# A bias that VectorE works out in one operation where ScalarE took two, and five changed slots, in a top-k attention and two mixture layers

## The chip, the cores and the metric

The kernel runs on one core of a Trainium2 chip. The metric is the device time of one execution in microseconds, as the median of several runs. Engines are named as in the profile: PE is TensorE, DVE is VectorE, ACT is ScalarE, POOL is GpSimd, SP issues most DMAs.

## The reference, cut to what matters

```python
# q, k, v: (2, 8, 576, 64); top_k 32
scores = scale * np.matmul(q, k.transpose(0, 1, 3, 2))
kth = np.partition(scores, -top_k, axis=-1)[..., -top_k:-top_k + 1]
mask = scores >= kth
scores = np.where(mask, scores, -1000000000.0)
scores = scores - np.max(scores, axis=-1, keepdims=True)
attn = np.exp(scores)
attn = attn / (np.sum(attn, axis=-1, keepdims=True) + 1e-09)
x = np.matmul(attn, v)                      # then to 1152 tokens x 512
...
for e in range(4):                          # first layer, gates p
    out += p[:, e:e + 1] * (np.maximum(x @ w1[e], 0.0) @ w2[e])
...
h = np.maximum(np.maximum(x @ m1, x @ m2), x @ m3)   # second layer
return h @ mo
```

## The kernel before, in words

**Work.** The 1152 tokens are nine tiles of 128 rows. For each tile and each of four pairs of heads there is one "pair" of attention work, 36 in all, numbered n from 0 (tiles 0 to 3 in order, then tiles 4 and 5 mixed, then 6 to 8). A pair has two heads, j = 0 and j = 1. The result of a pair is a slice `xl`, `xh` (a value in two parts) of a tile's `x`, written at lines L630 and L631. Expert work (the first layer, lines L776 to L778, three matmuls for one product) needs whole tiles: stage c of it, for c from 1 to 6, multiplies tiles c-1 and c with half of the first layer's weights, and needs the four slices of tile c.

**One head of one pair.** PE makes the scores (L477 to L489), ACT copies them to `s` (L501). DVE then finds the 32 largest of 576 scores by seven operations, i = 0 to 6: MAX8 (eight largest, L519) for even i, MATCH_REPLACE8 (with a MATCH_VALUE_LOAD, L521) for odd i. `m[:, 0]` is the largest value, `m[:, 31]` the 32nd, which is known after i = 6. The masked exponential is made on ACT for the heads in `ON_ACT`, which are j = 0 of pairs 2 to 35 and j = 1 of pairs 2, 5, 6, 8, 9, 10, 12, 13 and 14: `negate` (L526) puts -scale times the largest into `nb`; `mask` runs a Prelu (L540) that multiplies what lies under the 32nd value's side by a huge or tiny factor, an Identity (L541) that makes the bias `nb` = scale * kth + nb, and the Exp with that bias and a running sum (L542). For the other heads ACT makes the Exp (L533) and DVE or POOL multiplies by the mask (L547). PE transposes the result (`psp`, L565, L570), ACT copies it (`pt`, L568, L573), PE multiplies with v (`psv`, L607, L610). The sums go through `guard` (ACT, L578), `recip` (DVE, L584), `spread` (ACT, L588), a transpose (`psr`, PE, L593) and a copy `r` (ACT, L595). `norm` (DVE, L617) makes `xt`, ACT `xh` (L630), POOL `xl` (L631).

**Order.** The engines run their instructions in program order. The order is written in slots: pair n begins at slot 8n, and a table of options says at which slot after that each step is issued. `stag` is the delay of j = 1 against j = 0, `at` the slots of the two transposes, `lag` the slots between a PE step and the ACT copy of its result, `rec` that of `recip`, `guard` by default one before, `pv` that of the product with v, `turn` that of `trans_r`. BOTH holds for pairs 8, 9, 10, 12, 13 and 14, SECOND for pair 7, THIRD for pair 11, LOOSE for pairs 15 to 35. Top-k operations of a slot are put ahead of the rest of it. Slots are taken as their steps come up, so a slot lasts about two top-k operations on DVE.

**Filling.** Between two slots the program issues expert work for PE up to a planned time: `clock["goal"]` rises by what `dve(n)` adds for each DVE operation (0.07 us and n/960 us). A stage of expert work is not issued before the slot in which its newest tile's last slice is. When no expert work can be issued, the slot passes without any.

Other names that come up: L269 and L275 split weights in two parts (ACT, then POOL or DVE), L921 and L923 do the same for hidden values, L393 and L394 for k.

Of the kernel before, what the change touches and what calls it, by code (L numbers as in the profile page):

```python
# [10 lines left out]
F32 = mybir.dt.float32  # L11
# [3 lines left out]
AF = mybir.ActivationFunctionType  # L15
ALU = mybir.AluOpType
PSUM = bass.MemoryType.PSUM

TOPK = 32
# [19 lines left out]
FIRST = dict(stag=2, new=1, scores=-12, trans=11, pv=17, rec=16, lag=2, sum=4, late=1)  # L39
MIDDLE = dict(stag=2, new=1, scores=-12, at=(11, 12), pv=14, rec=12, lag=1, sum=0, late=1)  # L40
TIGHT = dict(stag=3, new=1, scores=-7, at=(10, 11), guard=11, rec=11, spread=12, pv=12, turn=12, norm=13, split=13, last=14, lag=0, lag_s=1, sum=0, late=1)
SECOND = dict(TIGHT, rec=12, norm=14, split=14, last=15)
THIRD = dict(stag=4, new=1, scores=-4, at=(11, 12), guard=12, rec=13, spread=13, pv=14, turn=14, norm=15, split=15, last=16, lag=0, lag_s=2, sum=0)
BOTH = dict(stag=4, new=1, scores=-4, at=(14, 14), pv=17, rec=15, lag=2, lag_t=1, sum=0, late=1)
LOOSE = dict(stag=4, new=1, scores=-4, at=(14, 14), pv=17, rec=15, split=22, last=24, lag=2, sum=0)

EARLY = 7
SOONER = 3
# [13 lines left out]
def kernel(  # L62
# [14 lines left out]
    nc = tc.nc  # L77
    B, HP, D, _, S = k.shape
    NT, DM = out.shape
    E = gates.shape[2]  # L80
    P = 128
# [6 lines left out]
    SCALE = 1.0 / float(D) ** 0.5  # L88
# [24 lines left out]
    at = ctx.enter_context(tc.tile_pool(name="at", bufs=2))  # L113
# [17 lines left out]
    def dve(n):  # L131
        clock["dve"] += 0.07 + n / 960.0
# [318 lines left out]
    class Pair:  # L451
# [55 lines left out]
        def topk(self, j, i):  # L507
            if i == 0:
                if self.n or j:
                    self.m[j] = at.tile([P, TOPK], F32, tag="m%d" % j, name="m8")  # L510
                self.w[j] = at.tile([P, 2, SH], F32, tag="w%d" % j, bufs=1, name="work")
            assert ("s", j) in self.did
            dve(S)
            if self.n == j == i == 0:
                return
            m, r = self.m[j], i // 2
            src = self.s[j] if i <= 1 else self.w[j]
            if i % 2 == 0:
                nc.vector.max(m[:, 8 * r:8 * r + 8], src)  # L519
            else:  # L520
                nc.vector.match_replace(out=self.w[j], in_to_replace=m[:, 8 * r:8 * r + 8], in_values=src, imm_value=NEG)  # L521

        def negate(self, j):
            m = self.m[j]
            self.nb[j] = at.tile([P, 1], F32, tag="nb%d" % j, name="nb")
            nc.scalar.activation(out=self.nb[j], in_=m[:, 0:1], func=AF.Copy, scale=-SCALE)  # L526

# [7 lines left out]
        def mask(self, j):  # L535
            p = self.p[:, j].rearrange("p (a n) -> p a n", a=2)
            s, kth, total = self.s[j], self.m[j][:, TOPK - 1:TOPK], self.rs[:, j:j + 1]
            if self.on_act[j]:
                eb = self.nb[j]
                nc.scalar.activation(out=s, in_=s, func=AF.Prelu, scale=-1.0, bias=kth, alpha=1.0 / STEEP)  # L540
                nc.scalar.activation(out=eb, in_=kth, func=AF.Identity, scale=SCALE, bias=self.nb[j])  # L541
                nc.scalar.activation(out=p, in_=s, func=AF.Exp, scale=-SCALE * STEEP, bias=eb, accum_out=total)  # L542
                self.did.update([("p", j), ("sum", j)])
                return lambda: None
            if not self.on_pool[j]:
                dve(S)
                nc.vector.scalar_tensor_tensor(out=p, in0=s, scalar=kth, in1=p, op0=ALU.is_ge, op1=ALU.mult, accum_out=total)  # L547
                self.did.update([("p", j), ("sum", j)])
                return lambda: None
            nc.gpsimd.tensor_scalar(out=s, in0=s, scalar1=kth, scalar2=None, op0=ALU.is_ge)  # L550
            nc.gpsimd.tensor_tensor(out=p, in0=p, in1=s, op=ALU.mult)
            self.did.add(("p", j))

            def add():
                nc.scalar.activation(out=s, in_=p, func=AF.Copy, accum_out=total)
                self.did.add(("sum", j))
            return add
# [75 lines left out]
    def attention():  # L633
# [5 lines left out]
        def options(n):  # L639
            return TIGHT if n == HP - 1 else SECOND if n == 2 * HP - 1 else MIDDLE if n in (HP - 2, 2 * HP - 3, 2 * HP - 2) else FIRST if n < 2 * HP else THIRD if n == 3 * HP - 1 else BOTH if n in ON_ACT[1] else LOOSE  # L640

        def at_slot(s, f, *a):
            later.setdefault(s, []).append((f, a))
# [3 lines left out]
        for n, (c, hp, t) in enumerate(pairs):  # L647
# [8 lines left out]
            elif n and t < FULL:  # L656
                o = options(max(0, n - 2))
                at_slot(max(8 * n + options(n)["scores"] - LOAD_FULL, 8 * (n - 2) + o["scores"] + o["stag"] + 1), load_full, n)
        free = {"k": -99, "q": -99}
        for key, n in first_use.items():  # L660
# [3 lines left out]
            load, split = (load_k, split_k) if key[0] == "k" else (load_q, split_q)  # L664
            at = max(s0 + options(n)["scores"] - (SPLIT_K if key[0] == "k" else SPLIT_Q), free[key[0]] + 2)
            if key[0] == "k" and key[1] and key[2]:

                at = max(at, 8 * pairs.index((MIXED, key[2] - 1, MIXED)) + options(n)["scores"] + options(n)["stag"] + (1 if key[2] == HP - 1 else 4))
# [3 lines left out]
        for n, (c, hp, t) in enumerate(pairs):  # L672
            s0 = 8 * n
            prs[n] = Pair(n)
            pr = prs[n]
            o = options(n)
            if n == 2 * HP - 2:
                o = dict(o, guard=11, rec=13, spread=13, turn=14)

            def two(s, f, *a, lag=o["lag"]):  # L680
                if f == pr.scores and n > 2 * HP:
                    at_slot(s, lambda: later.setdefault(s + lag, []).insert(0, (f(*a), ())))
                    return
                at_slot(s, lambda: at_slot(s + lag, f(*a)))
            for j in range(2):
                b0 = s0 + o["stag"] * j
                two(b0 + o["scores"] - SOONER * ((t, hp) in later_scores) - (n == HP - 1 and not j), pr.scores, j, lag=o.get("lag_s", o["lag"]))
                for i in range(7):
                    if o["new"]:
                        later.setdefault(b0 + i, []).insert(0, (pr.topk, (j, i)))  # L690
                    else:
                        at_slot(b0 + i, pr.topk, j, i)
                at_slot(b0 + 2, pr.negate, j)
                at_slot(b0 + 5, pr.exp, j)
                late = o.get("late", MASK_LATE) * pr.on_act[j] + (n == 3 * HP and not j)
                two(b0 + 7 + late, pr.mask, j, lag=o["sum"] if n < EARLY else 3)
                two(s0 + o["at"][j] if "at" in o else b0 + o["trans"] + late + (late > 0), pr.trans_p, j, lag=o.get("lag_t", o["lag"]))
            two(s0 + o["at"][1] if "at" in o else s0 + o["stag"] + o["trans"], pr.trans_p, 2, lag=o.get("lag_t", o["lag"]))
            at_slot(s0 + o.get("guard", o["rec"] - 1), pr.guard)
            at_slot(s0 + o["rec"], pr.recip)  # L700
            if o is LOOSE:
                at_slot(s0 + o["rec"], at_slot, s0 + o["rec"] + 1, pr.spread)
            else:
                at_slot(s0 + o.get("spread", o["rec"] + 1), pr.spread)
            at_slot(s0 + o["pv"], pr.pv)
            two(s0 + o.get("turn", o["rec"] + 2), pr.trans_r)
            end = max(o["pv"], o["rec"] + 2) + o["lag"]
            if n == 1:
                at_slot(s0, nc.sync.dma_start, gate, gates)
            if n == HP - 1:  # L710
                between.setdefault(s0 + o["norm"], []).append((norm_gates, ()))
            if "norm" in o:
                between.setdefault(s0 + o["norm"], []).append((pr.norm, ()))
            else:
                at_slot(s0 + end + 1, pr.norm)
            two(s0 + o.get("split", end + 2), pr.split_x)
# [6 lines left out]
        last = {}  # L723
        for n, p in enumerate(pairs):
            o = options(n)
            last[p[0:2]] = 8 * n + o.get("last", max(o["pv"], o["rec"] + 2) + 2 * o["lag"] + 2)
        for n in range(len(alone)):
            at_slot(ALONE_FROM + ALONE_STEP * n, load_alone, n + 1)
        end = max(last.values()) + 1
        s = min(later)  # L730
        while s <= end:
            todo = later.pop(s, [])
            i = 0
            while i < len(todo):
                f, a = todo[i]
# [15 lines left out]
    lag = []  # L751
# [438 lines left out]
```

## Time and profile before

| | |
|---|---|
| median of the runs | 738.36 us |
| runs | 732.49, 738.36, 738.43 us |
| time of the profiled execution | 732.22 us |
| span of the profiled execution, first to last instruction | 730.4 us |
| granted TensorE clock over the span | 1.000 |
| PE busy (matmul) | 714.1 us, 98% |
| DVE busy | 578.5 us, 79% |
| ACT busy | 504.5 us, 69% |
| POOL busy | 477.7 us, 65% |

The profiled execution took 1.8 us more than its span, and 6.1 us less than the median. Busy shares are averages over the whole span: attention fills DVE until about 430 us, expert work fills PE until the end. Matmuls are pipelined and their ends are modelled, so the waits of an engine say more than its busy share.

### The profile page before, as it was taken

What the parts mean: (1) busy time and instruction counts of PE and PEld (TensorE: products, weight loads), DVE (VectorE), ACT (ScalarE), POOL (GpSimd) and SP (SyncE); (2) the same over time, 40 slices, a digit from 0 to 9 for tenths busy, and PEclk for the clock granted to TensorE, in tenths of its full rate; (3) what the DMA queues carried; (4) which work ended last, traced back from release to release, by engine and by line L of the source; (5) the groups of instructions that cost most, each with busy time, mean ns of one, the idle gap of its engine ahead of it and who ended that gap; (6) DMA issues with size and microseconds to landing.
All of it is one profiled execution on the core that took longest, in us unless ns stands there. A gap on an engine that the chain in (4) does not pass through costs nothing. (4 is left out here: it accounts for less than half of the span.)

```text
span 730.4 us, 13791 instructions
## 1 busy us (share of the span) xinstructions
PE 714.1 (98%) x4758; PEld 637.5 (87%) x4758; DVE 578.5 (79%) x1174; ACT 504.5 (69%) x1127; POOL 477.7 (65%) x416
## 2 busy tenths in 40 slices
PE   6999999999999999999999999999999999999997
PEld 3677688889999998899889998999898998998996
DVE  6999989989999999999999964776879873323441
ACT  4868989899987887788788876566556753442531
POOL 2514878678989976788879777866736763542520
PEclk9999999999999999999999999999999999999999
DMA  8995465545756553555455446886889856543501
GB/s 240 310 273 205 136 207 160 163 123 155 212 151 191 157 170 125 172 165 188 133 154 170 144 122 208 298 285 215 278 256 329 256 182 223 179 125 115 188 1 43
DMA packets 57813, 135.26 MB, mean 185 GB/s; under 512 B 9936, under 2 KB 23120, under 8 KB 57744
## 3 DMA queue, kind: packets, MB, share of 16 engines
q1 hardware_dynamic: 49248, 125.74, 54.7%
q10 hardware_dynamic: 8496, 8.65, 3.4%
q8 instruction: 37, 0.61, 0.3%
q14 instruction: 32, 0.26, 0.1%
HBM read 123.36 MB, written 11.01 MB: 184 GB/s over the span
## 5 line engine op out<-in xcount | busy, mean ns | idle before, releaser
L275 POOL TENSOR_TENSOR wlo<-raw,whi 128x512 fp32r<-128x512 f32 x252 | 332.4, 1348 | 137.5 <-ACT whi L269 120.2
L269 ACT ACTIVATE whi<-raw 128x1024 fp32r<-128x1024 f32 x164 | 169.6, 1057 | 18.3 <-PE ps L778 9.8
L776 PE MATMUL ps<-xl,whi 128*128 128x256 f32 (+1 forms) x584 | 173.7, 297 | 0.5 <-POOL xl L631 0.5
L778 PE MATMUL ps<-xh,wlo 128*128 128x256 f32 (+1 forms) x584 | 170.6, 292 | 0.0
L777 PE MATMUL ps<-xh,whi 128*128 128x256 f32 (+1 forms) x584 | 170.5, 292 | 0.0
L519 DVE MAX8 m<-work 128x8 f32<-128x576 f32 x216 | 154.9, 743 | 0.1
L776 PEld LDWEIGHTS ps<-xl,whi 128*128 128x128 f32 x584 | 110.7, 189 | 1.8 <-POOL xl L631 0.7
L777 PEld LDWEIGHTS ps<-xh,whi 128*128 128x128 f32 x584 | 109.7, 188 | 0.9 <-issue 0.2
L778 PEld LDWEIGHTS ps<-xh,wlo 128*128 128x128 f32 x584 | 109.6, 188 | 0.0
L521 DVE MATCH_REPLACE8 work<-m,work 128x576 f32<-128x576 f32 x144 | 106.5, 740 | 0.0
L275 DVE TENSOR_TENSOR wlo<-raw,whi 128x1024 fp32r<-128x1024 f32 x38 | 54.3, 1436 | 50.1 <-ACT whi L269 37.7
L776 PE MATMUL ps<-wlo,h 128*128 128x512 f32 x224 | 90.3, 403 | 0.0
L778 PE MATMUL ps<-whi,h 128*128 128x512 f32 x224 | 87.7, 392 | 0.0
L777 PE MATMUL ps<-whi,h 128*128 128x512 f32 x224 | 87.7, 391 | 0.0
L245 POOL TENSOR_TENSOR narrow<-narrow,raw 128x256 int32<-128x256 int32 x48 | 46.7, 979 | 21.3 <-DMA narrow<-narrow 5.5
L501 ACT ACTIVATE s<-pss 128x288 f32<-128x288 f32 x128 | 45.8, 405 | 14.2 <-PE pss L481 6.9
L519 DVE MAX8 m<-s 128x8 f32<-128x576 f32 x71 | 53.0, 746 | 1.9 <-ACT s L501 1.9
L521 DVE MATCH_REPLACE8 work<-m,s 128x576 f32<-128x576 f32 x72 | 53.3, 740 | 0.0
L568 ACT ACTIVATE pt<-psp 128x512 f32<-128x512 f32 x72 | 40.0, 599 | 16.6 <-PE psp L565 16.6
L1057 DVE TENSOR_TENSOR tm<-ps,tm 128x384 f32<-128x384 f32 x36 | 19.8, 556 | 39.0 <-PE ps L778 39.0
L778 PEld LDWEIGHTS ps<-whi,h 128*128 128x128 f32 x224 | 42.1, 188 | 9.8 <-POOL h L916 0.3
L776 PEld LDWEIGHTS ps<-wlo,h 128*128 128x128 f32 x224 | 42.7, 191 | 6.6
(118 smaller groups left out, 1493.0 us busy)
## 6 DMA issues: line engine op xcount, KB each, us to landing
raw<-in_w_dram SPq DMA_DIRECT2D x128, 512.0 KB, 4.2
raw<-narrow SPq DMA_DIRECT2D x36, 512.0 KB, 4.3
raw<-in_m_dram SPq DMA_DIRECT2D x36, 256.0 KB, 5.1
whole<-in_w_dram SPq DMA_DIRECT2D x14, 512.0 KB, 5.9
narrow<-narrow ACTq DMA_DIRECT2D x48, 128.0 KB, 5.2
kraw<-in_k_dram SPq DMA_DIRECT2D x16, 288.0 KB, 4.4
raw<-in_mo_dram SPq DMA_DIRECT2D x12, 256.0 KB, 5.6
kfull<-in_k_dram SPq DMA_DIRECT2D x9, 288.0 KB, 5.3
```

The source lines that it names most:

```text
L245: nc.gpsimd.tensor_tensor(out=out.bitcast(I32), in0=out.bitcast(I32), in1=last, op=ALU.add)
L269: nc.scalar.activation(out=hi, in_=raw, func=AF.Copy)
L275: on.tensor_tensor(out=lo[:, x], in0=raw[:, x], in1=hi[:, x].bitcast(F32), op=ALU.subtract)
L501: nc.scalar.activation(out=s[:, h, :], in_=halves[h][:, 0:SH], func=AF.Copy)
L519: nc.vector.max(m[:, 8 * r:8 * r + 8], src)
L521: nc.vector.match_replace(out=self.w[j], in_to_replace=m[:, 8 * r:8 * r + 8], in_values=src, imm_value=NEG)
L568: return lambda: [nc.scalar.activation(out=d, in_=ps.rearrange("p (r n) -> p r n", r=NR), func=AF.Copy), self.did.add(("pt", part))]
L776: nc.tensor.matmul(ps, lhsT=lh, rhs=rl, start=first, stop=False)
L777: nc.tensor.matmul(ps, lhsT=lh, rhs=rh, start=False, stop=False)
L778: nc.tensor.matmul(ps, lhsT=ll, rhs=rh, start=False, stop=last)
L1057: nc.vector.tensor_tensor(out=tm[:, g], in0=ps, in1=tm[:, g], op=ALU.max)
```

## The change

The options of five pairs or groups of pairs move. SECOND (pair 7) transposes the second head one slot earlier. BOTH keeps `guard` and the transposes where they were and puts `recip` one slot later. Pair 12 transposes at slot 15 (before, 14), and has its product with v and `trans_r` one slot later. The copy of the first scores of pair 8 goes to the front of its slot. `norm` and `split_x` of a pair that has an option `turn` take their slot from it, which puts those of pair 6 one slot earlier.

From pair 5 on (`BIAS`), for heads whose mask is on ACT, one DVE operation on a column, issued just after the last MAX8, makes the bias as (m[31] - m[0]) * scale; `negate` and the Identity of the mask are not issued for these heads. Each of these operations also adds `dve(1)`, 0.071 us, to the plan.

```diff
-SECOND = dict(TIGHT, rec=12, norm=14, split=14, last=15)
+SECOND = dict(TIGHT, at=(10, 10), rec=12, norm=14, split=14, last=15)
...
-BOTH = dict(stag=4, new=1, scores=-4, at=(14, 14), pv=17, rec=15, lag=2, lag_t=1, sum=0, late=1)
+BOTH = dict(stag=4, new=1, scores=-4, at=(14, 14), guard=14, pv=17, rec=16, spread=16, turn=17, lag=2, lag_t=1, sum=0, late=1)
...
+BIAS = 5
...
             if i % 2 == 0:
                 nc.vector.max(m[:, 8 * r:8 * r + 8], src)
+                if i == 6 and self.on_act[j] and self.n >= BIAS:
+                    self.nb[j] = at.tile([P, 1], F32, tag="nb%d" % j, name="eb")
+                    dve(1)
+                    nc.vector.tensor_scalar(out=self.nb[j], in0=m[:, TOPK - 1:TOPK], scalar1=m[:, 0:1], scalar2=SCALE, op0=ALU.subtract, op1=ALU.mult)
...
         def negate(self, j):
             m = self.m[j]
+            if self.on_act[j] and self.n >= BIAS:
+                return
...
                 nc.scalar.activation(out=s, in_=s, func=AF.Prelu, scale=-1.0, bias=kth, alpha=1.0 / STEEP)
-                nc.scalar.activation(out=eb, in_=kth, func=AF.Identity, scale=SCALE, bias=self.nb[j])
+                if self.n < BIAS:
+                    nc.scalar.activation(out=eb, in_=kth, func=AF.Identity, scale=SCALE, bias=self.nb[j])
...
             if n == 2 * HP - 2:
                 o = dict(o, guard=11, rec=13, spread=13, turn=14)
+            if n == 3 * HP:
+                o = dict(o, at=(15, 15), pv=18, turn=18)
 
             def two(s, f, *a, lag=o["lag"]):
-                if f == pr.scores and n > 2 * HP:
+                if f == pr.scores and (n > 2 * HP or n == 2 * HP and not a[0]):
...
-            end = max(o["pv"], o["rec"] + 2) + o["lag"]
+            end = max(o["pv"], o.get("turn", o["rec"] + 2)) + o["lag"]
...
-            last[p[0:2]] = 8 * n + o.get("last", max(o["pv"], o["rec"] + 2) + 2 * o["lag"] + 2)
+            last[p[0:2]] = 8 * n + o.get("last", max(o["pv"], o.get("turn", o["rec"] + 2)) + 2 * o["lag"] + 2)
```

## Rows read from the trace of the kernel before

**Rows 1.** Stretches: busy us (and instructions) of each engine, clock, DMA share.

```profile
65.00:147.40 82.40, 80.49 (x571) 66.01 (x569) 77.61 (x170) 73.15 (x186) 60.83 (x56) 1.00 0.51 148
...
280.00:430.00 150.00, 150.00 (x1124) 135.80 (x1124) 149.93 (x319) 120.25 (x280) 121.10 (x104) 1.00 0.50 155
430.00:616.00 186.00, 185.70 (x1091) 171.26 (x1091) 128.99 (x236) 112.20 (x211) 121.13 (x104) 1.00 0.73 243
```

**Rows 2.** Waits of PE from 65 us on: total us, times, longest us.

```profile
PE psp L565 <- ACT p L542: 1.1, 2, 0.8
PE psv L607 <- ACT pt L573: 1.0, 2, 0.7
PE ps L776 <- POOL xl L631: 0.5, 1, 0.5
PE pso L776 <- DVE wlo L275: 0.3, 1, 0.3
```

**Rows 3.** Timeline, stage 2's last slice (start, us, engine, [idle before]).

```profile
146.16 0.27 DVE L617 TENSOR_TENSOR xt<-psv,r 128x128 f32<-128x128 f32 x1
...
147.37 0.39 PE L776 MATMUL ps<-xl,whi 128*128 128x256 f32 x1 [0.51 <-POOL xl L631]
```

**Rows 4.** Timeline, stage 4's last slice.

```profile
277.55 0.27 DVE L617 TENSOR_TENSOR xt<-psv,r 128x128 f32<-128x128 f32 x1
...
278.24 0.46 POOL L631 TENSOR_TENSOR xl<-xt,xh 128x128 fp32r<-128x128 f32 x1
...
279.93 0.28 PE L776 MATMUL ps<-xl,whi 128*128 128x256 f32 x1
```

**Rows 5.** Groups of ACT's instructions by line: count, busy us, mean ns.

```profile
L526 ACT ACTIVATE nb<-m 128x1 f32<-128x1 f32 x72 | 14.1, 198 | 0.0
L541 ACT ACTIVATE nb<-m,nb 128x1 f32<-128x1 f32 x43 | 12.6, 294 | 0.0
```

**Rows 6.** Timeline of ACT, 76 to 82 us.

```profile
76.56 0.28 ACT L595 ACTIVATE r<-psr 128x128 f32<-128x128 f32 x1 [0.84 <-PE psr L593]
...
80.51 0.76 ACT L540 ACTIVATE s<-s,m 128x576 f32<-128x576 f32 x1
...
81.18 0.28 ACT L541 ACTIVATE nb<-m,nb 128x1 f32<-128x1 f32 x1
81.49 0.78 ACT L542 ACTIVATE p<-s,nb 128x576 f32<-128x576 f32 x1
```

**Rows 7.** Timeline of DVE, two places.

```profile
144.06 0.15 DVE L584 RECIPROCAL rr<-rs 128x2 f32<-128x2 f32 x1
144.13 1.39 DVE L519 MAX8 m<-work 128x8 f32<-128x576 f32 x2
...
427.58 0.76 DVE L519 MAX8 m<-work 128x8 f32<-128x576 f32 x1
428.38 0.09 DVE L521 MATCH_VALUE_LOAD work<-m,work 128x8 f32 x1
```

**Rows 8.** Waits of DVE from 65 to 147.4 us.

```profile
DVE m L519 <- ACT s L501: 1.9, 3, 0.9
DVE xt L617 <- ACT r L595: 1.3, 1, 1.3
DVE rr L584 <- ACT rs L578: 0.8, 1, 0.8
```

**Rows 9.** Timeline of DVE at 86 us.

```profile
86.75 0.76 DVE L519 MAX8 m<-s 128x8 f32<-128x576 f32 x1 [0.84 <-ACT s L501]
```

**Rows 10.** Timeline of PE, two waits.

```profile
94.19 0.49 PE L607 MATMUL psv<-pt,v_last 128*128 128x128 f32 x2 [0.74 <-ACT pt L573]
...
156.76 0.66 PE L565 MATMUL psp<-ident,p 128*128 128x128 f32 x4 [0.78 <-ACT p L542]
```

**Rows 11.** Waits of DVE from 147.4 to 280 us.

```profile
DVE h L923 <- ACT h L921: 4.5, 3, 2.6
...
DVE p L547 <- ACT p L533: 0.2, 1, 0.2
```

## The prediction, made before the changed kernel was run

> **What bounds the kernel now.** I read the stretches first. From 65 to 147.4 us, PE is busy for 80.5 of 82.4 us and DVE for 77.6; from 280 to 430 us both are full (150.0 and 149.9 of 150); from 430 us on DVE has 57 us to spare and PE has none [rows 1]. So PE's stream sets the end, and since the change leaves PE's work as it is, only PE's waits can move the time. There are few of them after 65 us, where the change begins: 1.1, 1.0, 0.5 and 0.3 us, 2.9 in all [rows 2]. The change can't win more than that, unless work that PE does is itself shorter, and nothing in the diff is.
>
> Next I asked what could make PE wait longer, which is attention coming late. Expert work of stage c can't start its fourth slice before the last pair of its newest tile has been written. For stage 2 that is pair 11: PE waits 0.51 us for its `xl` at 147.37 us. The step before, `xt` on DVE at 146.16 us, has no idle time ahead of it: its inputs lay ready and DVE came to it in its order [rows 3]. For stage 4 it is pair 21: `xt` at 277.55 us, again with no idle time ahead, `xl` done at 278.24 + 0.46 = 278.70 us, first used at 279.93 us [rows 4]. So stage 2 has no margin, stage 4 has 1.23 us, and both are paced by how far DVE has come in its own queue. The same difference for the other stages (their rows carry no term and are not shown) is some 4 us for stage 3 and tens of us for stages 5 and 6, and the last tile is finished after 430 us, where DVE has room [rows 1]. Two gates therefore decide: DVE's delay D at 146 us, and at 277.5 us.
>
> **What the bias removes and adds.** 39 heads change (31 of j = 0 and 8 of j = 1). On ACT, 39 of the 72 operations of L526 and 39 of the 43 of L541 go, of 198 and 294 ns each [rows 5]. ACT's instructions overlap, so the relief is what the next one starts earlier: Identity to Exp is 81.49 - 81.18 = 0.31 us [rows 6], and about 0.1 of an L526, half its mean, as such a small one hides in its neighbours. I take 0.4 us a head. ACT isn't what PE or DVE waits for at most places, so this counts only where DVE stands waiting for ACT.
>
> On DVE, 39 column operations come in. No row shows this operation. From below, a column operation that waits for nothing starts its successor 0.07 us later (144.06 to 144.13, rows 7). But this one reads what the MAX8 just ahead of it has written. The nearest row is a MATCH_VALUE_LOAD that reads the MAX8 right before it: it starts 428.38 - 427.58 = 0.80 us after it, where two MAX8 that don't depend on each other last 1.39 us together, one 0.73 to 0.76, so that the second starts 0.63 to 0.66 us after the first [rows 7]. The dependence costs 0.14 to 0.17 us. The price is 0.14 + 0.07, about 0.2 us; I keep 0.07 and 0.25 as ends, and take 0.2, since that row has the same producer. Pairs 5 to 11 and the first head of pair 12 come ahead of the first gate, 13 heads: 2.6 us. Up to pair 22, ahead of the second gate, it is 26 heads: 5.2 us.
>
> The Trainium skill, page "VectorE: DVE Perf Modes", section "The DRAIN you can't avoid", says that of eight copies in a row a semaphore after each costs nothing extra. By it the operation would cost 0.07 us and not 0.2; the pair of rows above differs from it by 0.14 us, so I go by the rows.
>
> **What DVE gets back ahead of the first gate.** Its waits there are 1.9 us for `s` in three, 1.3 for `r` and 0.8 for `rs` [rows 8].
> - The wait of 0.84 us at 86.75 us is for an ACT that has run without a pause since 76.56 us [rows 9, 6], with two Identities and one `negate` of the changed kind since then: 0.7 us back. The 0.9 us wait has a pause of ACT shortly ahead of it, for a weight's DMA, and stays. The third, the remaining 0.15 us, goes.
> - `recip` one slot later in BOTH: at pair 8 DVE waits 0.8 us for `rs`; with two top-k operations (1.3 us) put ahead of it the wait goes, 0.8 us back. Behind it on DVE nothing else is queued later than before. But `spread` on ACT, in the same slot, now waits for a `recip` that comes up to 1.3 us later at the other five pairs, and ACT's score copies are queued behind it. Bounds 0 to 1.3 us; I take 0, because ACT has 9 of 82 us free [rows 1].
> - Pair 7's second transposes a slot earlier: PE's wait of 0.74 us [rows 10] goes, because `p` is finished before PE's first four transposes end, and the ACT chain to `r` starts some 0.7 us sooner. Of DVE's 1.3 us wait for `r`, 0.7 us come back.
>
> Together 0.7 + 0.15 + 0.8 + 0.7 = 2.35 us. D at the first gate is 2.6 - 2.35 = +0.25 us: the slice of pair 11 comes 0.25 us later than before. PE arrives earlier, because it has lost its waits of 0.74 us and some 0.3 us upstream, and waits that much longer: what is won ahead of 147 us is eaten there.
>
> **Between the gates.** Pair 12's transposes now come a slot after `p` is done, and PE's wait of 0.78 us goes [rows 10]; the product with v and the turn, a slot later, hold nobody, since pair 12's slice is needed in stage 3, which has 4 us. PE stands at 0.25 - 0.8 = -0.55 us. DVE pays 13 more heads, 2.6 us, and gets back less: its 4.5 us for hidden values are three waits in which ACT is behind by about one mask each, 0.4 us, so 1.2, and 0.2 us for `p` [rows 11]. D at the second gate is 5.2 - 2.35 - 1.4 = +1.45 us, and less the margin of 1.23 us the slice is used 0.2 us later than before. PE waits 0.75 us there, and ends up at **+0.2 us**.
>
> **After it.** 13 heads more cost DVE 2.6 us in a stretch in which it is full, but the slices there have tens of us of margin, and what is late at 430 us falls into DVE's free time [rows 1]. If that cover were gone, up to 2.6 us would show. PE's last wait, 0.3 us for a weight [rows 2], I leave as it is.
>
> **Edits costed at nothing.** The copy of pair 8's first scores: no other ACT instruction of its slot stands ahead of it, so ACT's order stays. Pair 6's `norm` and `split_x` a slot earlier: their slice has some 4 us of margin; at 0. The plan's 0.071 us a head lets expert work run at most 26 x 0.071 = 1.8 us earlier in PE's queue, ahead of attention's matmuls; all the stage's work is issued before its gate in either case, and at both gates DVE's own order comes last [rows 3, 4], so 0, with 0 to +0.9 us as bounds. No DMA changes its place. On POOL, only `xl` of pairs 6 and 12 moves, by a slot.
>
> **Sum.** 0.25 - 0.8 + 0.75 = +0.2 us. The profiled execution takes 732.22 us (span 730.4 and 1.8 around it) and would take 732.4. The median is 6.1 us above it, and the three runs spread by 5.9 us without any change; nothing in the trace says from what, so I put the sum on the median: **738.6 us**. The measurement of this kernel tells about 1% from no change, 7.4 us, more than twice all of PE's waits.
>
> **Rivals.**
> 1. *The column operation costs 0.07 us, and PE keeps its gains.* Then DVE pays 26 x 0.07 = 1.8 us up to the second gate and gets 3.75 back: both slices come earlier, neither gate closes, and PE loses its first three groups of waits, 1.1 + 1.0 + 0.5 = 2.6 us [rows 2]: 735.8 us. For it: DVE's waits for ACT are real. Against it: the dependent pair in rows 7. The Trainium skill's section named above would give this case.
> 2. *Slower: the gate of stage 4 closes.* With 0.25 us a head, DVE pays 6.5 us by 277.5 us. If only the two edits of the slots give time back (0.8 + 0.7) and ACT's relief nothing, since ACT's pauses ahead of most of DVE's waits show that it waits for others too, D is 5.0 us and PE stands 5.0 - 1.23 = 3.8 us longer at the first use of pair 21: 742.2 us. It decides from the point where D at 277.5 us passes 1.23 us. For it: DVE is saturated. Against it: the unbroken run of ACT in rows 6.
> 3. *The Identity's removal doesn't do what it says.* The Exp then reads the Prelu's output directly and may have to wait for its end: Prelu to Exp is 0.98 us now, the Prelu alone takes 0.76 [rows 6], so 0.2 us may be saved, not 0.3. Five places of relief lose 0.1 us each: +0.5 us, 739.1 us.
>
> **How the numbers follow.** Forecast (both gates set by DVE, within 1 us of 738.6) 0.5; rival 1 0.22; rival 2 0.2; rival 3 0.08. The range goes up to 742.2, rival 2's time. Down, it has to take in rival 1 and that the median may fall where the lowest run lay: 732.49 with half of rival 1's gain is 731.2. Faster by over 1% (under 731.0) needs the low run's level and rival 1 together: a third of 0.22, 0.07. Slower by over 1% (above 745.7) needs rival 2 with twice its price: 0.04. The rest, 0.89, is within 1%.
>
> **What would show it.** In the profile after: L526 33 and L541 4 times; a TENSOR_SCALAR on DVE 39 times, with its successor 0.2 us later than it would be after the MAX8 alone; DVE's waits for `rs` at pair 8 and for `s` at 86.75 us gone; no wait of PE for pair 12's `p`; PE still waiting for `xl` of pair 11, longer than 0.51 us, and now for that of pair 21 too. If the second of these waits is missing, D was over-estimated and the time goes to rival 1; if it is over 2 us, to rival 2. Wrong altogether it would be if expert work were issued in an order that makes PE wait for banks or weights somewhere else, which none of the rows shows now, or if DVE's delay reached the end of attention and from there the last layer.

## The result, and the profile after

The changed kernel takes 742.34 us (median of six runs, 740.85 to 747.27); the kernel before took 735.32 us beside it (six runs, 732.30 to 738.43). The ratio on record is 1.0122, with an interval from 1.0075 to 1.0169 (the quotient of the two medians is 1.0095; ratios here are those on record, which need not be that quotient): slower by about 1%, where 738.6 us and no measurable change were forecast. The six runs of after lie at three heights (740.9, 743.7 and 747.2 us), for which no profile shows a reason, and the profiled one, 740.85 us with a span of 738.9, is one of the lowest. In the later comparisons, with 17 to 27 runs each, the kernel before has medians of 732.55 to 732.95 us; against these the change loses 1.3%.

Stretches of after, and of before the one that [rows 1] leave out: busy us (and instructions) of PE, PEld, DVE, ACT and POOL, then clock, DMA share, GB/s.

```profile
65.00:147.40 82.40, 79.10 (x559) 64.22 (x558) 77.75 (x177) 68.75 (x158) 60.30 (x54) 1.00 0.49 148
147.40:280.00 132.60, 128.37 (x995) 116.25 (x993) 125.86 (x275) 107.33 (x235) 113.41 (x98) 1.00 0.53 162
280.00:430.00 150.00, 148.05 (x1131) 133.12 (x1131) 148.12 (x326) 115.30 (x254) 119.47 (x103) 1.00 0.50 154
430.00:616.00 186.00, 186.00 (x1100) 171.29 (x1097) 137.11 (x252) 113.73 (x220) 125.22 (x109) 1.00 0.72 237
```

```profile
147.40:280.00 132.60, 131.78 (x1042) 119.86 (x1043) 126.39 (x271) 114.26 (x270) 115.55 (x100) 1.00 0.55 168
```

Beside [rows 1]: PE loses 1.4 us of busy time in the first stretch, 3.4 us between the gates (131.78 to 128.37) and, where it was full before, 2 us between 280 and 430 us. From 430 us on it is full as before, so what has been lost by then stays lost. Another 0.8 us is lost ahead of 65 us (55.71 to 54.95), where the change has hardly begun (its first column operation is at 65.1 us). ACT has 4.4 us less to do in the first stretch and 5.0 between 280 and 430 us, as the change promises, and neither PE nor DVE ends sooner for it. The clock is 1.00 throughout.

Waits of PE in after from 65 us on (total us, times, longest).

```profile
PE ps L787 <- DVE h L934: 1.7, 1, 1.7
PE ps L787 <- POOL xl L640: 1.4, 2, 1.1
PE ps L787 <- POOL wlo L277: 1.1, 2, 0.8
PE pss L491 <- POOL kT L396: 1.0, 1, 1.0
PE psp L574 <- DVE p L556: 0.9, 1, 0.9
PE psp L574 <- ACT p L551: 0.8, 1, 0.8
PE pss L491 <- ACT pt L577: 0.7, 2, 0.4
...
PE ps L787 <- ACT whi L271: 0.6, 1, 0.6
...
```

All twelve rows sum to 9.6 us where [rows 2] sum to 2.9: 6.7 of the 8.5 us by which the span grew are PE's waits. They are of many kinds: expert work waits for a slice (`xl`), for hidden values (`h`) and for weights (`wlo`, `whi`), attention for `kT`, `p` and `pt`. So most of the loss is not at the two gates.

Waits of DVE in after from 65 to 430 us.

```profile
DVE h L934 <- ACT h L932: 5.8, 5, 2.3
DVE p L556 <- ACT p L541: 2.1, 2, 1.6
DVE acc L851 <- PE ps L789: 1.5, 1, 1.5
DVE xt L626 <- POOL ql L422: 1.4, 1, 1.4
DVE xt L626 <- ACT r L604: 0.4, 1, 0.4
DVE rr L593 <- ACT rs L587: 0.3, 1, 0.3
```

The forecast gains are there: no row for `s` any more, `r` down from 1.3 to 0.4 and `rs` from 0.8 at pair 8 to nothing before 147 us [rows 8]. But the sum is 11.5 us, and in the kernel before the same stretch has 10.9. Something else has taken their place: 2.3 us for a hidden value, at 103 us. In the kernel before the longest wait for one ahead of the first gate is 0.7 us (at 100.70 us, shown below). Timeline of after:

```profile
99.96 0.69 DVE L934 SCALAR_TENSOR_TENSOR h<-ps,h 128x512 fp32r<-128x512 f32 x1
102.96 0.69 DVE L934 SCALAR_TENSOR_TENSOR h<-ps,h 128x512 fp32r<-128x512 f32 x1 [2.31 <-ACT h L932]
...
148.83 0.28 DVE L626 TENSOR_TENSOR xt<-psv,r 128x128 f32<-128x128 f32 x1
...
150.04 0.38 PE L787 MATMUL ps<-xl,whi 128*128 128x256 f32 x1 [1.10 <-POOL xl L640]
...
284.52 0.27 DVE L626 TENSOR_TENSOR xt<-psv,r 128x128 f32<-128x128 f32 x1
...
285.72 0.39 PE L787 MATMUL ps<-xl,whi 128*128 128x256 f32 x1 [0.29 <-POOL xl L640]
```

Two subtractions `h` stand next to each other and the second waits 2.31 us with top-k operations queued behind it. The two gates follow [rows 3, 4]: pair 11's slice is used at 150.04 us and no longer at 147.37, pair 21's at 285.72 and no longer at 279.93, and the second now makes PE wait. The delays are +2.67 and +5.79 us, where the prediction had +0.25 and +0.2. But PE's own waits at the gates are only 1.10 and 0.29 us (0.51 and none before), 0.9 of the 6.7 us; PE reaches the first gate 2.1 us later already (150.04 - 1.10 = 148.94 us, before 147.37 - 0.51 = 146.86).

The new operation and those removed, in after: count, busy us, mean ns.

```profile
L525 DVE TENSOR_SCALAR eb<-m 128x1 f32<-128x1 f32 x39 | 8.4, 215 | 1.4
L534 ACT ACTIVATE nb<-m 128x1 f32<-128x1 f32 x33 | 6.6, 202 | 0.0
L550 ACT ACTIVATE nb<-m,nb 128x1 f32<-128x1 f32 x4 | 1.2, 301 | 0.0
```

The counts 39, 33 and 4 are those foreseen. What one operation costs is not its 215 ns but how much later it lets the next one start; timeline of DVE in after:

```profile
96.80 0.74 DVE L521 MAX8 m<-work 128x8 f32<-128x576 f32 x1
97.58 0.21 DVE L525 TENSOR_SCALAR eb<-m 128x1 f32<-128x1 f32 x1
97.71 0.08 DVE L527 MATCH_VALUE_LOAD work<-m,work 128x8 f32 x1
```

Over all 39, the operation starts 0.777 us (median) after the MAX8 that it reads, an operation that doesn't read it 0.66 us after it, and the next one starts 0.13 us later: 0.777 - 0.66 + 0.13 = 0.25 us each, the upper end of the prediction's bounds.

### The profile page after: what moved, and what is told of

Same layout as the page of the kernel before. It is cut to its first block, busy times and chain, and to the rows that moved or that the text cites. A ratio compares the mean times of both kernels' runs of the same rounds, so it can differ in the third digit from the quotient of the medians.

```text
span 738.9 us, 13758 instructions
## 1 busy us (share of the span) xinstructions
PE 715.4 (97%) x4758; PEld 636.3 (86%) x4758; DVE 588.8 (80%) x1213; ACT 493.3 (67%) x1049; POOL 478.4 (65%) x416
## 4 chain that ended last, share of the span: by engine, by line
PE 71%; DVE 9%; POOL 6%; ACT 6%; issue 4%; DMA 3%; SPq 0%; POOLq 0%; ACTq 0%; DVEq 0%
PE ps L789 17%; PE ps L787 17%; PE ps L788 17%; DVE m L521 5%; POOL wlo L277 5%; DVE work L527 4%; PE psv L619 3%; PE psp L574 3%; PE pss L491 2%; PE psa L873 2%; ACT whi L271 2%; PE pso L787 2%; PE pso L788 2%; PE pso L789 2%; PE ps L888 1%
## 5 line engine op out<-in xcount | busy, mean ns | idle before, releaser
L277 DVE TENSOR_TENSOR wlo<-raw,whi 128x1024 fp32r<-128x1024 f32 x38 | 57.5, 1518 | 52.0 <-ACT whi L271 38.7
```

The source lines that it names most:

```text
L277: on.tensor_tensor(out=lo[:, x], in0=raw[:, x], in1=hi[:, x].bitcast(F32), op=ALU.subtract)
```

## The experiments

The first theory was the prediction's rival 2: price and saturation of DVE. Four kernels take the change apart.

**slots_only**: the slot edits without the bias.

```diff
-BIAS = 5
+BIAS = 99
```

> The changed slots alone; the bias is made on ScalarE by two operations, as before. Price theory (each column operation on VectorE takes 0.25 us of a queue that decides when stages 2 and 4 of the expert work can start): the loss goes, the run is within 2 us of the kernel before, and the slice of pair 11 is ready within 1 us of 147.3 us. Slot theory (the loss comes from the moved slots): it keeps most of the loss, 4 to 8 us.

Measured: 734.79 us beside 732.70, ratio 1.0040 (1.0007 to 1.0072). Its waits of PE from 65 us on and those of DVE from 65 to 430 us:

```profile
PE ps L787 <- DVE h L934: 1.5, 1, 1.5
...
DVE m L521 <- ACT s L503: 3.0, 6, 0.8
DVE xt L626 <- ACT r L604: 2.1, 2, 1.7
```

The slots alone give no gain, but a small loss, well short of the 4 to 8 us of the slot theory. The waits that they aim at do go, and are replaced: PE's 0.78 us for pair 12's `p` [rows 10] by 1.5 us for `h`, at 160.34 us, 3.6 us after the old place; DVE's for `rs` and `r` by more waits for `s` (six, where the kernel before has three) and 1.7 us for an `r` at 170.62 us. The 1.5 us wait for an `h` from DVE is in the other kernels with these slots too (1.54 us in no_plan, 1.74 in after), and in none of plan_only, bias_only and bias_no_plan, which have the slots of before.

**bias_only**: after, with the slots of before (SECOND, BOTH, pair 12 and `two` as they were; bias and planned time stay).

```diff
-SECOND = dict(TIGHT, at=(10, 10), rec=12, norm=14, split=14, last=15)
+SECOND = dict(TIGHT, rec=12, norm=14, split=14, last=15)
...
-BOTH = dict(stag=4, new=1, scores=-4, at=(14, 14), guard=14, pv=17, rec=16, spread=16, turn=17, lag=2, lag_t=1, sum=0, late=1)
+BOTH = dict(stag=4, new=1, scores=-4, at=(14, 14), pv=17, rec=15, lag=2, lag_t=1, sum=0, late=1)
...
-            if n == 3 * HP:
-                o = dict(o, at=(15, 15), pv=18, turn=18)
...
```

> The bias on VectorE alone, in the slots of before. Price theory: 39 x 0.25 = 9.7 us more on VectorE, the last MAX8 ends 8 to 11 us later than before, the run is 5 to 10 us slower than before. Slot theory: at most 2 us slower.

Measured: 740.02 us, ratio 1.0107 (1.0074 to 1.0141); first use of pair 21's slice at 284.87 us. The bias and its planned time lose nearly as much as the whole change.

**no_plan**: after, without the planned time.

```diff
                     self.nb[j] = at.tile([P, 1], F32, tag="nb%d" % j, name="eb")
-                    dve(1)
```

> The whole change without the 0.071 us that each column operation adds to the plan, so that expert work is issued where it was against attention. Price theory: within 2 us of the changed kernel. Plan theory (expert work issued up to 1.9 us earlier pushes attention back in the queues of the tensor, vector and scalar engines): 3 us or more of the loss come back.

Measured: 736.53 us, ratio 1.0057 (1.0032 to 1.0082). DVE does the same operations as in after, and the gates come at 146.77 and 281.10 us. Its waits of DVE from 65 to 430 us:

```profile
DVE h L933 <- ACT h L931: 2.5, 2, 2.0
...
```

Its four rows sum to 4.5 us in place of 10.9: so 6.4 of the 39 x 0.25 = 9.7 us that the operation costs are paid out of DVE's waits. In after they are not, and the only difference is a planned time, which no engine executes. The medians differ by 5.8 us (742.34 and 736.53), where the plan theory asked for 3 us or more.

**eb_later**: after, the operation issued behind the next top-k operation and not directly behind the MAX8; planned time kept.

```diff
+    held = []
...
-                    nc.vector.tensor_scalar(out=self.nb[j], in0=m[:, TOPK - 1:TOPK], scalar1=m[:, 0:1], scalar2=SCALE, op0=ALU.subtract, op1=ALU.mult)
+                    held.append(lambda e=self.nb[j], m=m: nc.vector.tensor_scalar(out=e, in0=m[:, TOPK - 1:TOPK], scalar1=m[:, 0:1], scalar2=SCALE, op0=ALU.subtract, op1=ALU.mult))
+                    return
...
+            while held:
+                held.pop(0)()
...
             if self.on_act[j]:
+                while held:
+                    held.pop(0)()
```

> The whole change, but each column operation is issued behind the next top-k operation, so that it doesn't read what the operation right before it wrote. If the price is the dependence (0.12 us ahead of it and 0.06 behind it): MAX8 keeps its 0.66 us and the column operation starts its successor after 0.07 us, vector time falls by 39 x 0.18 = 7 us, and most of the loss comes back (within 3 us of before). If the price is the operation itself: as the changed kernel.

Measured: 745.88 us, ratio 1.0151 (1.0098 to 1.0204). A miss: the operation is cheaper (0.66 us behind its predecessor, 0.12 us ahead of its successor), but the time doesn't fall. PE waits 3.5 us in two places for a `p` from DVE that after has once, with 0.9 us. The second place has a cause of its own, the mask's product on DVE:

```profile
343.83 6.13 DVE L562 SCALAR_TENSOR_TENSOR p<-s,m,p 128x576 f32<-128x576 f32 x1
```

This one operation lasts 6.13 us, where the 24 of its kind have a median of 0.90 us. PE then waits 2.64 and 0.80 us, and its granted clock is 0.50 (1.2 GHz) for the next 3.4 us, so some 5 us are lost at this one place. There are only four runs: 745.64, 746.11, 746.44 and 740.27 us, and the last is as fast as the fastest of after (740.85). So the kernel doesn't show what the move is worth with the plan in place, but no run of it is clear of after's loss.

Second theory: the planned time moves expert work, with its evacuations on ACT and DVE, ahead of attention. Rival: it is the operation, and the plan only adds to it.

**plan_only**: the kernel before, with nothing but the planned time of 0.071 us at the 39 places.

```diff
                 nc.vector.max(m[:, 8 * r:8 * r + 8], src)
+                if i == 6 and self.on_act[j] and self.n >= 5:
+                    dve(1)
```

> The kernel before with nothing but 0.071 us more in the plan at each of the 39 places: no instruction added, none removed, none moved in attention; expert work is issued up to 2.8 us earlier. Plan theory (work of the experts that is issued earlier puts its copies and subtractions ahead of attention's in the queues of the scalar and vector engines, and these stand there until the products are done): slower by 3 to 6 us, with more waits of VectorE for h. Price theory: within 1.5 us of before. Theory of both together (the plan hurts only where VectorE is late by its new operations): within 2 us too.

Measured: 739.84 us beside 732.95, ratio 1.0090 (1.0062 to 1.0119). No instruction is added to any engine, and three quarters of the loss are there; the gates come at 151.28 and 284.98 us. Timelines of DVE, first the kernel before, then plan_only:

```profile
100.70 0.69 DVE L923 SCALAR_TENSOR_TENSOR h<-ps,h 128x512 fp32r<-128x512 f32 x1 [0.72 <-ACT h L921]
101.31 0.08 DVE L521 MATCH_VALUE_LOAD work<-m,s 128x8 f32 x1
...
102.11 0.74 DVE L521 MATCH_REPLACE8 work<-m,work 128x576 f32<-128x576 f32 x1
102.77 0.68 DVE L923 SCALAR_TENSOR_TENSOR h<-ps,h 128x512 fp32r<-128x512 f32 x1
```

```profile
101.28 0.69 DVE L925 SCALAR_TENSOR_TENSOR h<-ps,h 128x512 fp32r<-128x512 f32 x1 [0.36 <-ACT h L923]
104.45 0.69 DVE L925 SCALAR_TENSOR_TENSOR h<-ps,h 128x512 fp32r<-128x512 f32 x1 [2.49 <-ACT h L923]
105.06 0.08 DVE L523 MATCH_VALUE_LOAD work<-m,s 128x8 f32 x1
...
133.74 0.69 DVE L925 SCALAR_TENSOR_TENSOR h<-ps,h 128x512 fp32r<-128x512 f32 x1 [2.05 <-ACT h L923]
```

Before, two top-k operations lie between the two subtractions, and the second finds its input ready. In plan_only both subtractions come first, and the top-k operations stand behind a wait of 2.49 us. At 133.74 us the same happens again, for 2.05 us, where the kernel before has no wait (131.19 us). What DVE waits for is in ACT's row, first of the kernel before, then of plan_only:

```profile
98.11 0.77 ACT L540 ACTIVATE s<-s,m 128x576 f32<-128x576 f32 x1
...
100.07 0.60 ACT L921 ACTIVATE h<-ps 128x512 fp32r<-128x512 f32 x1
...
101.52 0.59 ACT L921 ACTIVATE h<-ps 128x512 fp32r<-128x512 f32 x1
```

```profile
100.64 0.60 ACT L923 ACTIVATE h<-ps 128x512 fp32r<-128x512 f32 x1 [1.49 <-PE ps L780]
101.14 0.77 ACT L542 ACTIVATE s<-s,m 128x576 f32<-128x576 f32 x1
...
102.90 1.04 ACT L269 ACTIVATE whi<-raw 128x1024 fp32r<-128x1024 f32 x1
103.84 0.58 ACT L923 ACTIVATE h<-ps 128x512 fp32r<-128x512 f32 x1
```

The first `h` now stands ahead of a head's mask on ACT (and ACT idles 1.49 us for PE first), the second behind it and behind a weight's split. In the kernel before the mask comes ahead of both.

**bias_no_plan**: slots of before, bias on DVE, no planned time (bias_only without `dve(1)`).

```diff
                     self.nb[j] = at.tile([P, 1], F32, tag="nb%d" % j, name="eb")
-                    dve(1)
```

> The bias on VectorE in the slots of before, without the 0.071 us in the plan. Plan theory: within 3 us of before, as the whole change without them (+0.6%, +2.8 us in span); VectorE's waits between 65 and 430 us fall from 11 to under 7 us. Price theory: 5 us slower or more, as with them (+1.1%).

Measured: 735.20 us, ratio 1.0033 (1.0014 to 1.0053). Beside bias_only, 1.0107, the planned time costs 0.74%.

**no_bias**: slots of before; ACT's two operations are left out, nothing is added.

```diff
+BIAS = 5
...
+    column = const.tile([P, 1], F32, name="column")
+    nc.gpsimd.memset(column, 0.0)
...
+            if self.on_act[j] and self.n >= BIAS:
+                return
...
-                eb = self.nb[j]
+                eb = self.nb[j] if self.n < BIAS else column
...
-                nc.scalar.activation(out=eb, in_=kth, func=AF.Identity, scale=SCALE, bias=self.nb[j])
+                if self.n < BIAS:
+                    nc.scalar.activation(out=eb, in_=kth, func=AF.Identity, scale=SCALE, bias=self.nb[j])
```

> ScalarE's relief alone: in the slots of before, from the sixth pair on the two ScalarE operations of the bias are left out and the Exp takes a column of zeros, so that the exponentials are not shifted by the row's largest score but by its 32nd; nothing is added on VectorE and nothing in the plan. If ScalarE's relief is worth what the run without the plan's 0.071 us showed (6.5 us less waiting of VectorE): the slice of pair 11 is ready 2 us or more earlier, PE's waits shrink and the run is 1 to 3 us faster than before. If the relief is worth little: within 0.7 us of before.

Measured: 730.90 us, ratio 0.9968 (0.9943 to 0.9993). The relief of ACT by itself is worth 0.3%, and this kernel, whose exponentials are shifted by the 32nd score of a row and not by the largest, is the only one of the study that is faster than the one before. Where the 0.3% arises isn't shown: its profiled execution (732.24 us) is the slowest of its ten and has the span of before, 730.4 us.

**dve_extra**: the kernel before with the column operation added into an unused tile; ACT keeps its two operations.

```diff
+    spare = const.tile([P, 1], F32, name="spare")
...
+                if i == 6 and self.on_act[j] and self.n >= 5:
+                    nc.vector.tensor_scalar(out=spare, in0=m[:, TOPK - 1:TOPK], scalar1=m[:, 0:1], scalar2=SCALE, op0=ALU.subtract, op1=ALU.mult)
```

> VectorE's price alone: the kernel before, with the same column operation on VectorE at the 39 places, its result used by nobody; ScalarE keeps its two operations, the plan and the slots are those of before. Price theory: 39 x 0.25 = 9.7 us more on VectorE, the last MAX8 ends 6 to 10 us later, the run is 4 to 8 us slower. If VectorE's price is mostly hidden in its waits for ScalarE: the last MAX8 under 4 us later, the run under 2 us slower.

Measured: 736.07 us, ratio 1.0037 (1.0021 to 1.0053); 3.1 us by the medians, between its two theories. DVE's waits from 65 to 430 us fall from 10.9 to 5.8 us here too, with ACT's work unchanged. So DVE, when it is later, waits less whatever ACT does, and this is enough for most of what looks like relief in no_plan. Beside bias_no_plan (1.0033) the relief of ACT can't be told from nothing as long as DVE pays for it.

Three kernels ask where the planned time hurts, and in which direction; each diff is against plan_only.

**plan_first**: the planned time for pairs 5 to 12 alone.

```diff
-                if i == 6 and self.on_act[j] and self.n >= 5:
+                if i == 6 and self.on_act[j] and 5 <= self.n <= 12:
                     dve(1)
```

> The kernel before with the 0.071 us in the plan for pairs 5 to 12 alone (14 heads, 1.0 us), nothing else. Gate theory (what VectorE loses by operations for h that were moved two top-k operations ahead, before 147 us, makes stage 2 start late, and PE can't win that back): the slice of pair 11 is ready 3 to 4 us later than before, as with all 39, and the run is 3 to 5 us slower. Sum theory (the loss grows with the count over the whole of attention): a third of the loss of all 39, about 2 us.

Measured: 736.15 us beside 732.84, ratio 1.0031 (1.0008 to 1.0053); gates at 151.21 and 283.25 us. Timeline of DVE:

```profile
104.36 0.69 DVE L925 SCALAR_TENSOR_TENSOR h<-ps,h 128x512 fp32r<-128x512 f32 x1 [2.48 <-ACT h L923]
```

The same two subtractions, the same wait: 14 places of 0.071 us, 1.0 us of planned time in all, make the first gate 3.84 us late, as late as all 39 do (3.91 us). But the run loses only a third of what plan_only loses, so most of that arises behind the first gate. The time itself, 3.3 us by the medians and 2.3 by the ratio, doesn't tell the gate theory from the sum theory.

**plan_late**: for pairs 24 to 35 alone.

```diff
-                if i == 6 and self.on_act[j] and self.n >= 5:
+                if i == 6 and self.on_act[j] and self.n >= 24:
                     dve(1)
```

> The kernel before with the 0.071 us in the plan for pairs 24 to 35 alone (12 heads, 0.85 us), nothing else. Gate theory: the first use of pair 21's slice at 280 us is unchanged and so is the run, within 1.5 us. Sum theory: a third of the loss of all 39, about 2 us.

Measured: 733.87 us, ratio 1.0004 (0.9978 to 1.0029): nothing measurable, at pairs whose slices by the prediction's reading have tens of us to spare.

**plan_less**: at all 39 places, but taken from the plan.

```diff
-                    dve(1)
+                    clock["dve"] -= 0.07 + 1 / 960.0
```

> The kernel before with 0.071 us less in the plan at each of the 39 places, so that expert work is issued up to 2.8 us later against attention. Theory that only work issued too early hurts: VectorE waits no longer for h than before, the run within 1.5 us of before or faster. Theory that the slots fit one plan and every displacement hurts: 3 us slower or more.

Measured: 737.06 us, ratio 1.0074 (1.0033 to 1.0115), 4.2 us by the medians. Less planned time costs time too (4.2 us, where more costs 6.9), so it isn't that expert work comes too early on principle: the slots of the kernel before fit the plan that it had. The profiled execution took 745.57 us, and one place in it accounts for what it has beyond the median:

```profile
387.36 9.96 DVE L549 SCALAR_TENSOR_TENSOR p<-s,m,p 128x576 f32<-128x576 f32 x1
...
397.99 0.89 PE L567 MATMUL psp<-ident,p 128*128 128x128 f32 x4 [4.54 <-DVE h L925]
```

```profile
398.30:405.10 6.80, 5.43 (x26) 5.06 (x24) 6.80 (x16) 3.13 (x9) 0.51 (x2) 0.50 0.19 73
```

The mask's product, of which the 24 have a median of 1.16 us, lasts 9.96 us, as one does in eb_later. PE waits 4.54 us (put down to the `h` right behind it on DVE) and then 1.37 us, and its granted clock is 0.50 (1.2 GHz) from 398.3 to 405.1 us. The waits and half of the 5.43 us that PE is busy at that clock make 8.6 us, an estimate; the execution is 8.5 us above the median. In both kernels POOL splits weights almost without a pause beside the long operation; why it lasts so long was not tested. What the other runs lose, some 4 us, this profile doesn't say.

**bias_later**: the last run puts the two findings together. The slots of before, no planned time, and the operation moved as in eb_later.

```diff
-                    nc.vector.tensor_scalar(out=self.nb[j], in0=m[:, TOPK - 1:TOPK], scalar1=m[:, 0:1], scalar2=SCALE, op0=ALU.subtract, op1=ALU.mult)
+                    held.append(lambda e=self.nb[j], m=m: nc.vector.tensor_scalar(out=e, in0=m[:, TOPK - 1:TOPK], scalar1=m[:, 0:1], scalar2=SCALE, op0=ALU.subtract, op1=ALU.mult))
+                    return
...
```

> The slots of the kernel before, the bias on DVE as one column operation from the sixth pair on, no planned time for it, and the operation issued behind the next top-k operation (or ahead of the mask that needs it), not directly behind the last MAX8. The same without the move measured 1.0033 times the kernel before. Theory (with the plan in its place, DVE's added time is what is left of the loss): a column operation that doesn't wait for the MAX8 ahead of it costs 0.12 us and not 0.25; 26 of them ahead of the gate of stage 4 save 3.4 us of DVE, of which the waits of DVE for ACT give part back, so the last MAX8 ends 2 to 4 us earlier than 435.15 us, the first use of pair 21's slice at 280.0 to 280.8 us, and the ratio is 0.997 to 1.001. Rival (what the earlier run of a moved operation showed: the mask's bias comes later, the exponential with it, and DVE's saving turns into waits of PE for `p`): the last MAX8 at 435 us or later, PE waits for `p` over 2 us in sum, ratio 1.004 to 1.008.

Measured: 732.71 us beside 732.55, ratio 1.0005 (0.9997 to 1.0014). Timeline of DVE, and PE's waits from 65 us on:

```profile
97.43 0.74 DVE L528 MATCH_REPLACE8 work<-m,work 128x576 f32<-128x576 f32 x1
98.09 0.20 DVE L525 TENSOR_SCALAR eb<-m 128x1 f32<-128x1 f32 x1
98.21 0.75 DVE L522 MAX8 m<-s 128x8 f32<-128x576 f32 x1
```

```profile
PE ps L790 <- POOL xl L645: 0.9, 1, 0.9
...
PE psp L579 <- ACT p L556: 0.3, 1, 0.3
```

The operation starts 98.09 - 97.43 = 0.66 us after its predecessor, as an independent one does, and costs 0.12 us. The last MAX8 ends at 429.65 us (before 429.99, bias_no_plan 435.15), the gates come at 146.90 and 279.39 us, and nothing is left of the loss. The rival, waits of PE for `p`, is refuted: 0.3 us. So the move by itself does no harm; what eb_later lost belongs to what else it has: the plan's order, the moved slots and the one long operation.

The runs side by side: waits of PE from 65 us on and of DVE from 65 to 430 us are the sums of the rows of those views, the gates are the first uses of the slices of pairs 11 and 21. The span and the waits are those of the profiled execution, which is the slowest of ten in bias_no_plan (737.21 us, median 735.20) and the fastest in no_plan and bias_later; the ratio of after is against the six runs with the median of 735.32.

| kernel | ratio | span | waits of PE | waits of DVE | gates |
|---|---|---|---|---|---|
| before | 1 | 730.4 | 2.9 | 10.9 | 147.37, 279.93 |
| slots_only | 1.0040 | 732.1 | 4.5 | 11.6 | 146.35, 280.94 |
| dve_extra | 1.0037 | 734.0 | 4.3 | 5.8 | 149.02, 281.98 |
| plan_only | 1.0090 | 737.7 | 8.2 | 16.5 | 151.28, 284.98 |
| bias_only | 1.0107 | 737.8 | 8.6 | 10.4 | 150.86, 284.87 |
| after | 1.0122 | 738.9 | 9.6 | 11.5 | 150.04, 285.72 |
| no_plan | 1.0057 | 733.2 | 5.4 | 4.5 | 146.77, 281.10 |
| bias_no_plan | 1.0033 | 735.4 | 6.6 | 4.8 | 148.11, 280.83 |
| bias_later | 1.0005 | 730.0 | 2.4 | 7.2 | 146.90, 279.39 |

## Why the prediction was wrong

**What bounds the kernel** was read rightly. PE's busy time is about the same (714.1 before, 715.4 after), PE is full from 430 us on in both, and the time moves with PE's waits. That the two gates follow DVE's order held too: in every profile `xt` of pairs 11 and 21 has no idle time ahead of it. But "two gates therefore decide" did not hold: of the 6.7 us by which PE's waits grew, 0.9 are at the gates, and PE comes to the first one 2.1 us later, where the prediction had it come earlier.

**The step that failed** is among the edits costed at nothing: "The plan's 0.071 us a head lets expert work run at most 26 x 0.071 = 1.8 us earlier in PE's queue ... so 0, with 0 to +0.9 us as bounds." It measured +0.90% alone (plan_only, 6.9 us by the medians), 0.74% with the bias in place (1.0107 against 1.0033). The reason given was that DVE's order comes last at both gates and that the stage's work is issued before its gate anyway. Both hold, the second for PE's matmuls. But what the plan places is not only matmuls: each product brings its evacuations on ACT and DVE along, and these take places in the very order of DVE that decides the gates. A planned time that is some 0.4 us ahead by 100 us (six heads of 0.071) is enough to issue a product one place earlier; its subtraction then stands ahead of two top-k operations and waits 2.3 us in after and 2.5 us in plan_only. The bound was made from the size of the shift, and the price is that of a product that changes its place. The prediction even named this as what would make it "wrong altogether", expert work issued in another order, and gave it no price; a loss of over 1% had a chance of 0.04.

**The price of the column operation**, 0.2 us, measured 0.25: 26 x 0.05 = 1.3 us too little by the second gate. The dependence was taken at 0.14 us or a little more and is 0.12, the step to the next operation at 0.07 and is 0.13. The bounds held. By the Trainium skill, page "VectorE: DVE Perf Modes", section "The DRAIN you can't avoid", a semaphore behind each of eight copies adds nothing; here the dependent place costs 0.25 us and the independent one 0.12, so for this pair the trace differs, as the prediction took it. It matters: bias_no_plan and bias_later, which differ in that place alone, have 1.0033 and 1.0005 (their intervals just touch, at 1.0014).

**What DVE gets back** came where it was forecast: `s` at 86.75 us, `rs` at pair 8, and 0.8 of the 1.27 us for `r` of pair 7 are gone. The sum was even too small: in no_plan DVE's waits fall by 6.4 us up to 430 us, where 3.75 were counted up to the second gate. The cause was partly another one: dve_extra, with ACT as busy as before, gets 5.1 us back. Without the plan the forecast of the gates was fair: -0.6 and +1.2 us in no_plan, +0.25 and +0.2 forecast.

**Between the gates**, PE's wait of 0.78 us for pair 12 goes, and "holds nobody" failed: 1.5 us for `h` at 160 us come in its place. DVE's waits for `s`, which the prediction saw as possible behind a later `spread` and took at 0 of 0 to 1.3 us, are 3.0 us in slots_only where they were 1.9; that `spread` makes them was not tested. The slots cost 0.4% alone. Beside the bias without the plan (1.0057 against 1.0033) the intervals overlap.

**After the second gate**, DVE's delay was put down to free time behind 430 us, "up to 2.6 us would show" if that cover were gone. In after PE loses 2 us between 280 and 430 us, in rows of `wlo`, `pt`, `xl` and `h`: mostly late weights and evacuations, not late slices (0.29 us for `xl`). So that the price named is near the 2 us is luck: it was that of another way to lose time.

**The base.** The sum was put on the median of three runs, 738.36 us. With more runs the kernel before has 732.6 to 733.0, near its profiled execution; the profile's own time was the better base, and the choice hid 5 to 6 us of the miss.

**The rivals.** Rival 2 had the direction, and its 742.2 us is next to the 742.34 measured, but that is luck: by it PE stands 3.8 us longer at pair 21's slice, and PE waits 0.29 us there. And bias_no_plan, which has its price and not the plan, loses 0.3% only. Rival 1's cheap operation exists, in bias_later, and there PE keeps 0.5 us, not 2.6.

**What stays open.** plan_first (0.31%) and plan_late (0.04%) don't add up to plan_only (0.90%); the heads of pairs 13 to 23, or the places together, were not tried by themselves. One row points there: after, bias_only, plan_only and eb_later, the kernels with all 39 planned times added, each have a wait of PE of 0.9 to 1.1 us for `kT` at 246 to 247 us, and no other kernel has it. How the moved products lead to it was not followed. Nor were the slots of after tried with the moved operation and without the plan.

## What to carry to other kernels

Where a program fills one engine's gaps by planned times, an edit of a planned time can move work on every engine that serves the filler: cost it by the product that may change its place (here waits of 2 us), not by its own 0.07 us, and try it alone, without the instruction that it stands for. A small operation that reads the result of the one just ahead of it pays for that place; let one other operation of the same engine lie between and half of the price is gone (0.25 to 0.12 us, 0.3% of this kernel). When an operation moves from a relieved engine to a full one, weigh the two halves apart: ACT's relief alone was worth 0.3%, DVE's burden alone cost 0.4% in the dear place, and together they cost 0.3% there and nothing measurable in the cheap place.

## What was unexpected of the hardware

A column operation of DVE lasts 0.20 to 0.21 us in the trace wherever it stands, yet takes 0.25 us of DVE's time behind the MAX8 that it reads and 0.12 us one operation later: its start is what moves (0.777 and 0.66 us after its predecessor's start), and the row's duration shows nothing of it. And a full engine pays for added work first with its own waits: of 9.7 us added in dve_extra 5.1 came out of them, so the added work shows in the time by less than its price. Last, one operation of a kind can last far longer than the others: 9.96 and 6.13 us for a mask's product on DVE in plan_less and eb_later, with medians of 1.16 and 0.90.
